# Decoding the first eight weight parts without the guard for tiny numbers, and looking through them late

## The chip, the cores and the metric

The kernel runs on one core of a Trainium2 chip. The metric is the device time of one execution in microseconds; the median of three runs is what a version is compared by. A profiled execution is a further one, taken by the hardware profiler, and has a time of its own.

## The reference

```
scores = 0.125 * q @ k.T, with a bias by distance and head, masked to
         8 global columns and a band of 96 columns; a = softmax(scores)
x = (a @ v), heads side by side                  # 1536 tokens x 512
h = maximum(x @ w_in, 0);   x = h*h @ w_out      # 512 -> 2048 -> 512
gate = 1 / (1 + exp(-(x @ w_gate)));  val = x @ w_val
out = (gate * val) @ w_out2                      # 512 -> 1536 -> 512
```

Two batches, eight heads, 768 positions, head size 64. The weights arrive as float64, so each number is two 32-bit words, and the kernel must make float32 of them on the chip.

## The kernel before

All work is a list of tasks. Each task names its engine (or a choice of two), an estimated duration, a rank, and the buffers that it reads and writes. A planner (`_Plan.issue`) walks through them in a modelled time: whenever an engine is free it takes, of the tasks whose inputs are ready by then, the one of lowest rank. The resulting order is the order of each engine's queue; on the chip every queue runs strictly in order, and an instruction that waits holds all that stands behind it. A load is taken to land its own estimate plus 2 us (`late=2000`) after its issue.

**Attention.** For each of twelve 128-row blocks, TensorE makes scores (L473), VectorE adds the bias and takes the row's extreme (L486), ScalarE takes the exponential (L491), ScalarE or VectorE divide (L510, L512), TensorE transposes (L523), ScalarE or VectorE copy the transposes out (tile `ats`), and TensorE multiplies by the values (L535). The result goes to tile `x` in two parts, a rounded high part and the rest.

**The two feed-forward layers.** Every product is made of three matmuls (L615 to L617): high by low, high by high, low by high. The first layer is done in four passes over its sixteen blocks of hidden columns, the second in four passes over twelve. Pass 0 of the first layer works in pieces of 256 tokens and is interleaved with the attention, since it needs only the `x` of two 128-row blocks; the later passes run 512 tokens at a time. Pass 0 needs the first eight of 68 weight parts: four of `w_in` (tile `h` is written from them), then four of `w_out` (tile `y`).

**A weight part** (`load_weight`) is 128 x 512 numbers, 512 KB. SyncE's queue starts its load into `wst`, a ring of two (L576). Then, in this order:

- L583, ScalarE: the absolute value of the high words, taken as float32, into `wu`
- L585, VectorE: the maximum of that and the smallest high word allowed, into `wx` (a ring of two); this is the guard for tiny numbers
- L587, VectorE: shift left by 5 and right by 2, in place
- L589, VectorE: bring in the top three bits of the low word, in place
- L592, VectorE: bring in the sign and the top exponent bit from the high word, in place
- L253, ScalarE: the rounded high copy into tile `w`
- L263, VectorE: `wx` less the high copy, into the second half of `w`

The words lie in pairs in `wst`, so a reader of the high words alone steps over every other word. The first eight parts go to buffers of pool `sb`; the other thirteen buffers lie in pool `late`, which is opened when the attention's tiles are given up.

**The general way.** L373 to L383 (`whether`) test the two numbers of the inputs that set the band, and write `gen_i`; at the end of the program every engine reads `gen_i` (L56) and, were it not zero, would run a slow way that covers all inputs.

Of the kernel before, what the change touches and what calls it, by code (L numbers as in the profile page):

```python
# [9 lines left out]
F32 = mybir.dt.float32  # L10
# [7 lines left out]
P = 128  # L18
# [4 lines left out]
FAR = 2.0 ** 38  # L23
F64_TOP = -(1 << 30)
F64_MIN = 2.0 ** -15 * 1.125


@with_exitstack
def kernel(
    ctx: ExitStack,  # L30
    tc: tile.TileContext,
    qw: bass.AP,
    kw: bass.AP,
    vw: bass.AP,
    nums: bass.AP,
    w1: bass.AP,
    w2: bass.AP,
    out: bass.AP,
):
    nc = tc.nc  # L40
    NT, DM = out.shape
    NQ, _, H, _ = qw.shape
    w1, w2 = w1.bitcast(I32), w2.bitcast(I32)
    slopes = [2.0 ** (-8.0 * (h + 1) / H) for h in range(H)]

    pers = ctx.enter_context(tc.tile_pool(name="pers", bufs=1))
    nf = pers.tile([P, 2], F32, name="nf")
    gen_i = pers.tile([P, 1], I32, name="gen_i")
    ident = pers.tile([P, P], F32, name="ident")

    with tc.tile_pool(name="sb", bufs=1) as sb, tc.manual_schedule():
        _fast(tc, sb, qw, kw, vw, nums, w1, w2, out, nf, gen_i, ident, slopes)

    engines = [mybir.EngineType.PE, mybir.EngineType.Activation, mybir.EngineType.DVE,
               mybir.EngineType.Pool, mybir.EngineType.SP]
    general = nc.values_load(gen_i[0:1, 0:1], engines=engines)  # L56
    with tc.If(general != 0):
        _general(tc, qw, kw, vw, w1, w2, out, nf, ident, slopes)
# [151 lines left out]
            t["fn"](t["e"]) if t["told"] else t["fn"]()  # L210


def _fast(tc, sb, qw, kw, vw, nums, w1, w2, out, nf, gen_i, ident, slopes):
    nc = tc.nc
    NT, DM = out.shape
    NQ, _, H, _ = qw.shape
# [25 lines left out]
    def act(n):  # L242
        return 200 + n * 0.83
# [31 lines left out]

    v, g = nc.vector, nc.gpsimd
    consts = buf("sb", [P, 1], F32, "consts")
    ni = buf("early", [P, 2, 2], I32, "ni")
    add("sp", 700, -1e6, lambda: nc.sync.dma_start(
        out=ni.ap, in_=nums.rearrange("(o a) b -> o a b", o=1).to_broadcast([P, 2, 2])),  # L280
# [9 lines left out]
    def setup():  # L290
# [82 lines left out]
        def whether():  # L373

            ok = early["sb"].tile([P, 1], F32, name="ok")
            ok2 = early["sb"].tile([P, 1], F32, name="ok2")
            v.tensor_scalar(ok, nl, 1.0, None, op0=ALU.is_ge)
            v.tensor_scalar(ok2, nl, float(NL_MAX), None, op0=ALU.is_le)
            v.tensor_tensor(ok, ok, ok2, op=ALU.mult)
            v.tensor_scalar(ok2, ng, float(GS), None, op0=ALU.is_le)  # L380
            v.tensor_tensor(ok, ok, ok2, op=ALU.mult)
            v.tensor_scalar(ok, ok, -1.0, 1.0, op0=ALU.mult, op1=ALU.add)
            v.tensor_copy(gen_i, ok)  # L383

        add("dve", 1300, 1e8, whether, r=[num], w=[(consts, "gen"), (small, "ok")])

    zero = buf("early", [P, TN], mybir.dt.bfloat16, "zero")
    scrap = buf("psb", [P, TN], F32, "h", 2)
# [178 lines left out]
    def load_weight(n, rank):  # L567
        key = chunks[n]
        k = n % (NA + NB)
        pool_name, bufs, tag = ("sb", NA, "wa") if k < NA else ("late", NB, "wb")  # L570
        st = buf("sb", [P, TN, 2], I32, "wst", 2)
        xx = buf("sb", [P, TN], F32, "wx", 2)
        u = buf("sb", [P, TN], F32, "wu", 1)
        t = buf(pool_name, [P, 2, TN], F32R, tag, bufs, f"w{n}")
        src = (w1 if key[0] == "a" else w2)[key[1], key[2]]
        add("sp", dma(P * TN * 8), rank - LEAD - 6000, lambda: nc.sync.dma_start(  # L576
            out=st.ap.rearrange("p n t -> p (n t)"), in_=src), w=[st], late=2000)
        lo, hi = (lambda: st[:, :, 0]), (lambda: st[:, :, 1])
        xi = lambda: xx.ap.bitcast(I32)
        rank -= LEAD  # L580


        add("act", act(TN), rank, lambda: nc.scalar.activation(u.ap, hi().bitcast(F32), ACTF.Abs),  # L583
            r=[st], w=[u])
        add("dve", dve(TN, False), rank, lambda: v.tensor_scalar(  # L585
            xx.ap, u.ap, F64_MIN, None, op0=ALU.max), r=[u], w=[xx])
        add("dve", dve(TN, False), rank, lambda: v.tensor_scalar(  # L587
            xi(), xi(), 5, 2, op0=ALU.logical_shift_left, op1=ALU.logical_shift_right), w=[xx])
        add("dve", dve(TN), rank, lambda: v.scalar_tensor_tensor(  # L589
            xi(), lo(), 29, xi(), op0=ALU.logical_shift_right, op1=ALU.bitwise_or),  # L590
            r=[st], w=[xx])
        add("dve", dve(TN), rank, lambda: v.scalar_tensor_tensor(  # L592
            xi(), hi(), F64_TOP, xi(), op0=ALU.bitwise_and, op1=ALU.bitwise_or), r=[st], w=[xx])
        copy(WHI, TN, rank, lambda: t[:, 0], lambda: xx.ap, [xx], [(t, 0)])
        minus(WLO, TN, rank, lambda: t[:, 1], lambda: xx.ap, lambda: f32(t[:, 0]), [xx, (t, 0)],
              [(t, 1)])
        made.append(t)


    clock = {"rank": CLK}  # L600
# [169 lines left out]
        rank += NTILE * 3 * len(fs) * KC * steps  # L770
    for n in range(len(chunks)):
        load_weight(n, when[n])
    for fn, p, *rest in work:
        clock["pace"] = 2.0 if fn is moe1 and p == 0 else 1.0
        fn(p, *rest)
# [229 lines left out]
```

## Time and profile before

| | us |
|---|---|
| median of 3 runs (lowest, highest) | 688.71 (688.39, 688.76) |
| the profiled execution | 689.12 |
| its span, first to last instruction | 687.2 |
| TensorE (PE) busy | 667.9 |
| VectorE (DVE) busy | 432.1 |
| ScalarE (ACT) busy | 285.7 |

The span is cut into the attention's opening, in which TensorE is short of work, a long middle in which it is hardly idle, and a last few microseconds of output. The profile names an engine's idle time by the instruction behind it and by what released that instruction. The granted clock of TensorE is given for a stretch as a share of 2.4 GHz: 1.00 is full, 0.50 is 1.2 GHz.

### The profile page before, as it was taken

The page shows a single profiled execution, that of the slowest core. Times are in us where ns is not written, and L with a number is a line of the kernel's source. Part 1 is how long each engine was busy: PE and PEld are TensorE (multiplying, and loading weights), DVE is VectorE, ACT ScalarE, POOL GpSimd, SP SyncE. Part 2 cuts the span into 40 slices and gives each one's busy share as a digit, 9 for nine tenths or more (in the row PEclk, how much of TensorE's full clock was granted, in tenths as well). Part 3 has the DMA queues.
Part 4 walks back from the last instruction along what each step waited for, and adds up shares of the span by engine and source line. Part 5 has one row for each costly group of instructions (what it writes and reads, how often), then busy time and mean ns, then how long its engine had stood idle before and what let it go on. Part 6 is the DMA issues. An engine that isn't in the chain of part 4 may idle for free.

```text
span 687.2 us, 10016 instructions
## 1 busy us (share of the span) xinstructions
PE 667.9 (97%) x3864; PEld 558.7 (81%) x3864; DVE 432.1 (63%) x976; ACT 285.7 (42%) x622; POOL 1.1 (0%) x8
## 2 busy tenths in 40 slices
PE   9878999999999999999999999999999999999996
PEld 7766899899988888888888888888888888888884
DVE  5878876768888888888857852476348223222232
ACT  5767777764463444554434541352113111211110
POOL 0000000000000000000000000000000000000000
PEclk9988899999999999999999999999999999999999
DMA  7754433201332332333210230043001000001011
GB/s 181 171 153 139 150 114 107 73 3 63 123 122 78 107 123 87 98 96 119 82 41 32 93 122 1 31 126 120 0 1 62 1 1 0 1 0 62 0 62 66
DMA packets 29335, 51.71 MB, mean 75 GB/s; under 512 B 3808, under 2 KB 16352, under 8 KB 29280
## 3 DMA queue, kind: packets, MB, share of 16 engines
q1 hardware_dynamic: 29280, 51.00, 24.4%
q8 instruction: 32, 0.52, 0.3%
q14 instruction: 23, 0.19, 0.1%
HBM read 47.84 MB, written 3.15 MB: 74 GB/s over the span
## 4 chain that ended last, share of the span: by engine, by line


## 5 line engine op out<-in xcount | busy, mean ns | idle before, releaser
L615 PE MATMUL h<-x,w 128*128 128x512 f32 (+1 forms) x528 | 197.8, 375 | 0.0
L617 PE MATMUL h<-x,w 128*128 128x512 f32 (+1 forms) x528 | 195.7, 371 | 0.0
L616 PE MATMUL h<-x,w 128*128 128x512 f32 (+1 forms) x528 | 195.7, 371 | 0.0
L615 PEld LDWEIGHTS h<-x,w 128*128 128x128 f32 x528 | 99.9, 189 | 17.5 <-issue 0.2
L617 PEld LDWEIGHTS h<-x,w 128*128 128x128 f32 x528 | 99.9, 189 | 16.9
L616 PEld LDWEIGHTS h<-x,w 128*128 128x128 f32 x528 | 100.0, 189 | 16.7
L713 DVE TENSOR_TENSOR r<-h,r 128x512 f32<-128x512 f32 x36 | 24.9, 691 | 103.1 <-PE h L617 101.6
L615 PE MATMUL y<-g,w 128*128 128x512 f32 (+1 forms) x240 | 86.3, 360 | 2.6 <-ACT w L253 1.7
L616 PE MATMUL y<-g,w 128*128 128x512 f32 (+1 forms) x240 | 84.3, 351 | 0.0
L617 PE MATMUL y<-g,w 128*128 128x512 f32 (+1 forms) x240 | 84.3, 351 | 0.0
L263 DVE TENSOR_TENSOR g<-r,g 128x512 fp32r<-128x512 f32 x84 | 57.7, 687 | 17.2 <-ACT g L253 16.7
L710 ACT ACTIVATE r<-h 128x512 f32<-128x512 f32 x36 | 21.5, 598 | 109.7 <-PE h L617 109.6
L583 ACT ACTIVATE wu<-wst 128x512 f32<-128x512 f32 x68 | 45.2, 665 | 48.5 <-DMA wst<-in_w_dram 41.1
L263 DVE TENSOR_TENSOR w<-wx,w 128x512 fp32r<-128x512 f32 x68 | 46.5, 685 | 21.2 <-ACT w L253 20.7
L615 PE MATMUL o<-w,g 128*128 128x512 f32 x144 | 56.9, 395 | 0.0
L616 PE MATMUL o<-w,g 128*128 128x512 f32 x144 | 56.9, 395 | 0.0
L617 PE MATMUL o<-w,g 128*128 128x512 f32 x144 | 56.8, 394 | 0.0
L253 ACT ACTIVATE w<-wx 128x512 fp32r<-128x512 f32 x68 | 42.5, 626 | 34.0 <-DVE wx L592 28.9
L253 ACT ACTIVATE g<-r 128x512 fp32r<-128x512 f32 x32 | 20.2, 632 | 82.5 <-DVE r L713 82.5
L615 PEld LDWEIGHTS y<-g,w 128*128 128x128 f32 x240 | 45.6, 190 | 10.5 <-ACT w L253 2.0
L617 PEld LDWEIGHTS y<-g,w 128*128 128x128 f32 x240 | 45.7, 190 | 6.7 <-DVE w L263 0.2
L616 PEld LDWEIGHTS y<-g,w 128*128 128x128 f32 x240 | 45.7, 191 | 6.4
(79 smaller groups left out, 827.5 us busy)
## 6 DMA issues: line engine op xcount, KB each, us to landing
wst<-in_w_dram SPq DMA_DIRECT2D x68, 512.0 KB, 3.5
k<-in_kw_dram SPq DMA_DIRECT2D x24, 128.0 KB, 2.9
q<-in_qw_dram SPq DMA_DIRECT2D x24, 128.0 KB, 3.1
vv<-in_vw_dram SPq DMA_DIRECT2D x12, 256.0 KB, 2.9
out_dram<-oacc SPq DMA_DIRECT2D x11, 256.0 KB, 2.1
vv<-in_vw_dram SPq DMA_DIRECT2D x10, 192.0 KB, 3.4
vv<-in_vw_dram SPq DMA_DIRECT2D x10, 64.0 KB, 2.8
out_dram<-oacc SPq DMA_DIRECT2D x2, 128.0 KB, 3.6
```

The lines of the kernel that those rows point to most:

```text
L253: nc.scalar.activation(to(), of(), ACTF.Copy)
L263: nc.vector.tensor_tensor(to(), of(), less(), op=ALU.subtract)
L583: add("act", act(TN), rank, lambda: nc.scalar.activation(u.ap, hi().bitcast(F32), ACTF.Abs), r=[st], w=[u])
L615: nc.tensor.matmul(p, lhsT=ww[:, 0, ws], rhs=lo, start=first, stop=False)
L616: nc.tensor.matmul(p, lhsT=ww[:, 0, ws], rhs=hi, start=False, stop=False)
L617: nc.tensor.matmul(p, lhsT=ww[:, 1, ws], rhs=hi, start=False, stop=last)
L710: add("act", act(TN), rk, lambda r=r, pt=pt: nc.scalar.activation(r.ap, pt.ap, ACTF.Sigmoid), r=[pt], w=[r])
L713: add("dve", dve(TN), rk, lambda r=r, pt=pt: v.tensor_tensor(r.ap, pt.ap, r.ap, op=ALU.mult), r=[pt], w=[r])
```

## The change

For parts 0 to 7 the absolute value and the maximum are gone: the shift reads the high words of `wst` itself. For all parts the sign comes in before the low word's bits, and those go to a new buffer `wf` (one of it): the high copy is made from `wx` without them, and the subtraction takes `wf` instead of `wx`.

After all weights, with a rank above that of any other work but `whether` and the fillers, each of the eight parts is loaded once more (`look_through`): ScalarE takes the absolute value, and VectorE sums what is below the guard into one column of `tiny`. Then (`decide`) a DMA lays `tiny`'s 128 x 8 sums into one row, `asked`; behind them stands the answer of `whether`, which no longer writes `gen_i`. VectorE sums the row, compares with zero and writes `gen_i`.

```diff
--- before.py
+++ after.py
@@ -23,6 +23,7 @@
 FAR = 2.0 ** 38
 F64_TOP = -(1 << 30)
 F64_MIN = 2.0 ** -15 * 1.125
+TINY = 8
 
 
 @with_exitstack
@@ -44,12 +45,13 @@
     slopes = [2.0 ** (-8.0 * (h + 1) / H) for h in range(H)]
 
     pers = ctx.enter_context(tc.tile_pool(name="pers", bufs=1))
+    asked = pers.tile([1, P * TINY + 1], F32, name="asked")
     nf = pers.tile([P, 2], F32, name="nf")
     gen_i = pers.tile([P, 1], I32, name="gen_i")
     ident = pers.tile([P, P], F32, name="ident")
 
     with tc.tile_pool(name="sb", bufs=1) as sb, tc.manual_schedule():
-        _fast(tc, sb, qw, kw, vw, nums, w1, w2, out, nf, gen_i, ident, slopes)
+        _fast(tc, sb, qw, kw, vw, nums, w1, w2, out, nf, gen_i, ident, slopes, asked)
 
     engines = [mybir.EngineType.PE, mybir.EngineType.Activation, mybir.EngineType.DVE,
                mybir.EngineType.Pool, mybir.EngineType.SP]
@@ -210,7 +212,7 @@
             t["fn"](t["e"]) if t["told"] else t["fn"]()
 
 
-def _fast(tc, sb, qw, kw, vw, nums, w1, w2, out, nf, gen_i, ident, slopes):
+def _fast(tc, sb, qw, kw, vw, nums, w1, w2, out, nf, gen_i, ident, slopes, asked):
     nc = tc.nc
     NT, DM = out.shape
     NQ, _, H, _ = qw.shape
@@ -275,6 +277,9 @@
 
     v, g = nc.vector, nc.gpsimd
     consts = buf("sb", [P, 1], F32, "consts")
+
+
+    tiny = buf("sb", [P, TINY], F32, "tiny")
     ni = buf("early", [P, 2, 2], I32, "ni")
     add("sp", 700, -1e6, lambda: nc.sync.dma_start(
         out=ni.ap, in_=nums.rearrange("(o a) b -> o a b", o=1).to_broadcast([P, 2, 2])),
@@ -380,9 +385,9 @@
             v.tensor_scalar(ok2, ng, float(GS), None, op0=ALU.is_le)
             v.tensor_tensor(ok, ok, ok2, op=ALU.mult)
             v.tensor_scalar(ok, ok, -1.0, 1.0, op0=ALU.mult, op1=ALU.add)
-            v.tensor_copy(gen_i, ok)
-
-        add("dve", 1300, 1e8, whether, r=[num], w=[(consts, "gen"), (small, "ok")])
+            v.tensor_copy(asked[:, P * TINY:], ok[0:1])
+
+        add("dve", 1300, 1e8, whether, r=[num], w=[(tiny, "asked"), (small, "ok")])
 
     zero = buf("early", [P, TN], mybir.dt.bfloat16, "zero")
     scrap = buf("psb", [P, TN], F32, "h", 2)
@@ -570,7 +575,6 @@
         pool_name, bufs, tag = ("sb", NA, "wa") if k < NA else ("late", NB, "wb")
         st = buf("sb", [P, TN, 2], I32, "wst", 2)
         xx = buf("sb", [P, TN], F32, "wx", 2)
-        u = buf("sb", [P, TN], F32, "wu", 1)
         t = buf(pool_name, [P, 2, TN], F32R, tag, bufs, f"w{n}")
         src = (w1 if key[0] == "a" else w2)[key[1], key[2]]
         add("sp", dma(P * TN * 8), rank - LEAD - 6000, lambda: nc.sync.dma_start(
@@ -579,22 +583,56 @@
         xi = lambda: xx.ap.bitcast(I32)
         rank -= LEAD
 
-
-        add("act", act(TN), rank, lambda: nc.scalar.activation(u.ap, hi().bitcast(F32), ACTF.Abs),
-            r=[st], w=[u])
-        add("dve", dve(TN, False), rank, lambda: v.tensor_scalar(
-            xx.ap, u.ap, F64_MIN, None, op0=ALU.max), r=[u], w=[xx])
-        add("dve", dve(TN, False), rank, lambda: v.tensor_scalar(
-            xi(), xi(), 5, 2, op0=ALU.logical_shift_left, op1=ALU.logical_shift_right), w=[xx])
-        add("dve", dve(TN), rank, lambda: v.scalar_tensor_tensor(
-            xi(), lo(), 29, xi(), op0=ALU.logical_shift_right, op1=ALU.bitwise_or),
-            r=[st], w=[xx])
+        shift = dict(op0=ALU.logical_shift_left, op1=ALU.logical_shift_right)
+        if n < TINY:
+            add("dve", dve(TN, False), rank, lambda: v.tensor_scalar(xi(), hi(), 5, 2, **shift),
+                r=[st], w=[xx])
+        else:
+
+            u = buf("sb", [P, TN], F32, "wu", 1)
+            add("act", act(TN), rank, lambda: nc.scalar.activation(
+                u.ap, hi().bitcast(F32), ACTF.Abs), r=[st], w=[u])
+            add("dve", dve(TN, False), rank, lambda: v.tensor_scalar(
+                xx.ap, u.ap, F64_MIN, None, op0=ALU.max), r=[u], w=[xx])
+            add("dve", dve(TN, False), rank, lambda: v.tensor_scalar(xi(), xi(), 5, 2, **shift),
+                w=[xx])
         add("dve", dve(TN), rank, lambda: v.scalar_tensor_tensor(
             xi(), hi(), F64_TOP, xi(), op0=ALU.bitwise_and, op1=ALU.bitwise_or), r=[st], w=[xx])
+
+        full = buf("sb", [P, TN], F32, "wf", 1)
+        add("dve", dve(TN), rank, lambda: v.scalar_tensor_tensor(
+            full.ap.bitcast(I32), lo(), 29, xi(), op0=ALU.logical_shift_right,
+            op1=ALU.bitwise_or), r=[st, xx], w=[full])
         copy(WHI, TN, rank, lambda: t[:, 0], lambda: xx.ap, [xx], [(t, 0)])
-        minus(WLO, TN, rank, lambda: t[:, 1], lambda: xx.ap, lambda: f32(t[:, 0]), [xx, (t, 0)],
-              [(t, 1)])
+        minus(WLO, TN, rank, lambda: t[:, 1], lambda: full.ap, lambda: f32(t[:, 0]),
+              [full, (t, 0)], [(t, 1)])
         made.append(t)
+
+    def look_through(n):
+
+        st = buf("sb", [P, TN, 2], I32, "wst", 2)
+        u = buf("sb", [P, TN], F32, "wu", 1)
+        src = w1[chunks[n][1], chunks[n][2]]
+        add("sp", dma(P * TN * 8), 1e7, lambda: nc.sync.dma_start(
+            out=st.ap.rearrange("p n t -> p (n t)"), in_=src), w=[st], late=2000)
+        add("act", act(TN), 1e7, lambda: nc.scalar.activation(
+            u.ap, st[:, :, 1].bitcast(F32), ACTF.Abs), r=[st], w=[u])
+        add("dve", dve(TN) + 80, 1e7, lambda: v.scalar_tensor_tensor(
+            u.ap, u.ap, F64_MIN, u.ap, op0=ALU.is_lt, op1=ALU.mult, accum_out=tiny[:, n:n + 1]),
+            w=[u, (tiny, n)])
+
+    def decide():
+
+        add("sp", 700, 1e7, lambda: nc.sync.dma_start(
+            out=asked[:, 0:P * TINY], in_=tiny.ap), r=[(tiny, n) for n in range(TINY)],
+            w=[(consts, "asked")], late=2000)
+
+        def fn():
+            v.tensor_reduce(asked[:, P * TINY:], asked, axis=AX.X, op=ALU.add)
+            v.tensor_scalar(asked[:, P * TINY:], asked[:, P * TINY:], 0.0, None, op0=ALU.is_gt)
+            v.tensor_copy(gen_i[0:1], asked[:, P * TINY:])
+
+        add("dve", 1600, 1e7, fn, r=[(tiny, "asked"), (consts, "asked")], w=[(consts, "gen")])
 
 
     clock = {"rank": CLK}
@@ -770,6 +808,9 @@
         rank += NTILE * 3 * len(fs) * KC * steps
     for n in range(len(chunks)):
         load_weight(n, when[n])
+    for n in range(TINY):
+        look_through(n)
+    decide()
     for fn, p, *rest in work:
         clock["pace"] = 2.0 if fn is moe1 and p == 0 else 1.0
         fn(p, *rest)
```

## Rows read from the trace of the kernel before

**Rows 1.** The page's first line.

```profile
span 687.2 us, 10016 instructions
```

**Rows 2.** Busy time, instructions, granted clock, DMA share and GB/s by stretch.

```profile
0.00:85.00 85.00, 73.40 (x692) 61.44 (x692) 66.14 (x254) 57.84 (x175) 1.09 (x8) 0.90 0.60 160
85.00:160.00 75.00, 74.68 (x811) 67.62 (x810) 55.06 (x194) 51.58 (x154) 0.00 (x0) 1.00 0.23 68
160.00:530.00 370.00, 369.12 (x1709) 306.45 (x1708) 265.95 (x465) 154.12 (x258) 0.00 (x0) 1.00 0.25 80
530.00:687.20 157.20, 150.66 (x659) 123.14 (x657) 44.93 (x66) 22.18 (x37) 0.00 (x0) 0.99 0.06 21
```

**Rows 3.** The same by finer stretches of the opening.

```profile
47.00:52.00 5.00, 5.00 (x28) 4.63 (x30) 3.16 (x10) 2.29 (x6) 0.00 (x0) 0.50 0.35 122
...
68.00:77.00 9.00, 7.28 (x44) 6.56 (x43) 7.58 (x28) 6.01 (x16) 0.00 (x0) 0.62 0.46 142
```

**Rows 4.** TensorE's order of time: start, us, line, tiles, [idle before <-releaser].

```profile
26.09 1.09 PE L535 MATMUL o<-ats,vv 128*64 128x128 f32 x16
...
45.38 0.41 PE L523 MATMUL at<-ident,sa 128*128 128x128 f32 x2 [2.11 <-DVE sa L512]
46.97 0.69 PE L523 MATMUL at<-ident,sa 128*128 128x128 f32 x2 [1.18 <-ACT sa L510]
...
51.00 1.86 PE L535 MATMUL o<-ats,vv 128*64 128x128 f32 x16
...
69.77 0.58 PE L615 MATMUL y<-g,w 128*128 128x256 f32 x1 [1.72 <-ACT w L253]
```

**Rows 5.** ScalarE's order of time around TensorE's two long waits.

```profile
43.85 0.66 ACT L583 ACTIVATE wu<-wst 128x512 f32<-128x512 f32 x1 [2.54 <-DMA wst<-in_w_dram]
...
46.42 0.89 ACT L510 ACTIVATE sa<-sa,sm 128x256 f32<-128x256 f32 x2
...
68.54 0.66 ACT L583 ACTIVATE wu<-wst 128x512 f32<-128x512 f32 x1 [1.20 <-DMA wst<-in_w_dram]
69.10 0.62 ACT L253 ACTIVATE w<-wx 128x512 fp32r<-128x512 f32 x1
```

**Rows 6.** VectorE's order of time at the same places.

```profile
43.78 0.18 DVE L498 RECIPROCAL sm<-sm 128x4 f32<-128x4 f32 x1
44.54 0.43 DVE L585 TENSOR_SCALAR wx<-wu 128x512 f32<-128x512 f32 x1 [0.58 <-ACT wu L583]
44.88 0.35 DVE L512 TENSOR_SCALAR sa<-sa,sm 128x256 f32<-128x256 f32 x1
...
66.77 0.68 DVE L592 SCALAR_TENSOR_TENSOR wx<-wst,wx 128x512 int32<-128x512 int32 x1
...
69.23 0.43 DVE L585 TENSOR_SCALAR wx<-wu 128x512 f32<-128x512 f32 x1 [1.18 <-ACT wu L583]
```

**Rows 7.** Groups of the decoding from 20 to 85 us.

```profile
L589 DVE SCALAR_TENSOR_TENSOR wx<-wst,wx 128x512 int32<-128x512 int32 x9 | 6.2, 685 | 0.0
...
L583 ACT ACTIVATE wu<-wst 128x512 f32<-128x512 f32 x9 | 6.0, 664 | 4.2 <-DMA wst<-in_w_dram 4.2
...
L263 DVE TENSOR_TENSOR w<-wx,w 128x512 fp32r<-128x512 f32 x8 | 5.5, 686 | 1.0 <-ACT w L253 0.8
...
L585 DVE TENSOR_SCALAR wx<-wu 128x512 f32<-128x512 f32 x9 | 3.8, 420 | 3.9 <-ACT wu L583 3.9
L587 DVE TENSOR_SCALAR wx<-wx 128x512 int32<-128x512 int32 x9 | 3.8, 420 | 0.0
```

**Rows 8.** SyncE's last weight loads and output, then the weight loads' landing.

```profile
162.22 358.67 SPq L576 DMA_DIRECT2D wst<-in_w_dram  x56
629.88 52.17 SPq L745 DMA_DIRECT2D out_dram<-oacc  x13
...
DMA to landing us min/median/max: 3.3/3.5/6.6
```

**Rows 9.** VectorE's order of time in the last pass but one.

```profile
573.50 0.69 DVE L713 TENSOR_TENSOR r<-h,r 128x512 f32<-128x512 f32 x1 [3.37 <-PE h L617]
```

## The prediction

> **What bounds the kernel now.** I read the stretches first. From 85 us to the end TensorE is the bound: it is idle for 0.32 us up to 160, for 0.88 up to 530, and for 6.54 after that, most of it the output behind the last matmul [rows 2]. A VectorE or ScalarE instruction that is saved there buys nothing, and one that is added costs nothing until it makes TensorE wait. The first 85 us are different: TensorE is idle for 85 - 73.40 = 11.6 us, its clock is granted at 0.90 on the mean, and VectorE is busy for 66 of the 85 us [rows 2]. The eight parts that lose their guard are decoded just there, between the instructions of the attention. So I looked at TensorE's waits in that stretch. The two largest places are 3.29 us around 45 us (2.11 for the divided scores of VectorE, then 1.18 for those of ScalarE) and 1.72 us before 69.77, for a weight part's high copy [rows 4]. After both TensorE runs at 1.2 GHz: granted 0.50 from 47 to 52 us, 0.62 on the mean from 68 to 77 [rows 3]. What that costs is seen on the sixteen value matmuls of a half block: 1.09 us at 26.09 in full clock, 1.86 at 51.00 [rows 4].
>
> **What the change takes out of these places.** ScalarE and VectorE show why TensorE waits [rows 5, 6].
>
> At 43.85 ScalarE begins L583 after 2.54 us of waiting for a weight load. Behind it in its queue stand an exponential, a piece of the feed-forward layer, a high copy, and only then, at 46.42, the division L510 that TensorE wants. That division's other input, the reciprocal, was ready at 43.78 + 0.18 = 43.96. Without L583 the queue is 2.54 us plus one instruction's pitch (68.54 to 69.10, so 0.56 us) further, 3.1 us, and L510 is then held by the reciprocal and the four short instructions ahead of it: about 44.2, 2.2 us earlier. On VectorE L585 waited 0.58 us for L583, with the division L512 behind it at 44.88; this goes as well. I count 2.0 us of the 3.29.
>
> At 68.54 ScalarE begins the next such L583, after 1.20 us of waiting for a load, and the copy that TensorE wants stands behind it at 69.10. Its data were ready when L592 ended, at 66.77 + 0.68 = 67.45. Without L583 it starts about 67.6, and the new order, in which the copy doesn't need the low bits, can give another VectorE slot. I count 1.5 us of the 1.72.
>
> The clock: from 47 to 52 us at half speed some 2.5 us are lost (5.00 us busy at 0.50), from 68 to 77 some 2.8 (7.28 us busy at 0.62, so 7.28 x 0.38) [rows 3]. Both losses follow a wait that shrinks without vanishing. No row says how short it must get for the clock to stay; the bounds are 0 and 5.3 us, and I take half, 2.6.
>
> VectorE's saved maximum: 8 x 0.34 us of queue (L585 at 44.54, L512 at 44.88 [rows 6]) is 2.7 us, of which the places above already hold some; I add 0.3 for the rest.
>
> **What it adds, on the path or beside it.** The shift now reads every other word of `wst`. No row has a one-source VectorE instruction on such a pattern. The bounds are 420 ns, as L587 takes on packed words, and 685 ns, as L589, a two-source one, takes on the same kind of pattern [rows 7]. L263, two-source on packed tiles, takes 686 ns, so the step costs nothing there; I take 420. At 685 the eight parts would cost 8 x 0.27 = 2.1 us of VectorE, and most of the 2.7 saved would be gone. The Trainium skill (SBUF — State Buffer, the note on cachelines under the port layout) says that a stride is free while two accesses fall into a line of 16 bytes, which 8 bytes between words satisfy. It agrees with L589 against L263; whether the faster one-source rate holds is shown by no run here.
>
> The load's wait moves from ScalarE to VectorE. Three L583 waited 4.2 us for loads in this stretch and three L585 waited 3.9 for L583 [rows 7], so VectorE pays most of it today. Loads land in 3.3 to 6.6 us, median 3.5 [rows 8], and the planner reckons with 3.5 (1.5 by size and the 2.0 of `late`), so a late one stalls the queue up to 3.1 us, with the scores' bias, the divisions and the reciprocals behind it. At 43.85 and at 68.54, where the loads came late, VectorE had other work until 44.0 and 68.1; I take no more waiting than today's, with 0 to 3.1 us for each late load as the bounds.
>
> For the 60 other parts the count of VectorE instructions stays, one buffer `wf` forces the next part's low-bit step behind the subtraction, and that behind the high copy. Most of it lies from 160 to 530 us, where TensorE waited 0.88 us in all [rows 2]: nothing.
>
> The looking through cannot start before the last weight load (162.22 + 358.67 = 520.9) has been decoded, near 530. Eight more loads through the ring of two, in four pairs of some 3.5 us plus L583 and one VectorE instruction (0.66 and 0.69 [rows 7]), take about 20 to 25 us; so it ends near 555. Then SyncE waits for the sums and sends them: a load's 3.3 to 6.6 us as bounds. VectorE's sum over 1025 numbers in one row is two L589 long, 1.4 us, and two short ones follow. All is over by some 565. Behind them on SyncE stand the outputs, the first at 629.88 [rows 8]; behind them on VectorE stand the gate's products. VectorE is idle for 3.37 us before one such product [rows 9] and has 44.93 us of work in the last 157 [rows 2]. The third product of a pass is wanted by TensorE only after two others' output matmuls, 24 of 150.66 / 659 = 0.229 us, so 5.5 us, of which product, copy and subtraction take about 2.1. An instruction of 1.4 us in the way is covered by the 3.4 left. If that cover were gone it would cost at most 1.4 us, three or four times. At the end the engines read `gen_i` as before, after 682: nothing.
>
> **The sum.** 2.0 + 1.5 + 2.6 + 0.3 = 6.4 us. TensorE's next waits in the opening, for the transposes' copies and the divisions that L583 doesn't hold up, are fed by the same loop of engines, and part of the gain will reappear there; a third is my choice, no row gives it. That leaves 4.3 us. The profiled execution took 689.12 us, its span 687.2 [rows 1] and 1.9 around it, so it would take 684.8; the median lies 0.4 under it, which gives **684.4 us**.
>
> **The rivals.**
>
> *The wait comes back (no change).* The loads are paced by the ring and by SyncE's order, and the attention by its own loop of scores, exponential and transpose; TensorE then waits as long, for something else, and the clock falls as often. For it: two more waits of that stretch are not behind L583. Against: the two largest are. Gain 0 to 1.4 us: 687.3 to 688.7, with as much above, so within 687.3 to 690.1.
>
> *VectorE blocks on the load (slower).* The planner puts the shift on VectorE at the modelled landing, one instruction sooner than L585 stood, and a late load holds VectorE instead of ScalarE. It decides from the point where a load lands over a microsecond after the queue has reached the shift. Three late loads of 1.2 to 2.5 us (the waits of [rows 5, 7]), less the 3.9 that VectorE waits today, would give little; but with all eight shifts meeting it, at 1 us each, less 3.9, and one more stretch at half clock of 2.5, VectorE loses 8 - 3.9 + 2.5 = 6.6 against the 2.7 saved: 3.9 us slower, 692.6; a milder case reaches from 690.1.
>
> *The clock stays up.* Both stretches of half clock vanish and the planner, with less work to place, fills the opening better: 6.4 + 2.7 more of clock = 9.1, so 679.6.
>
> *It doesn't do what it says:* a tiny number would send everything through the general way, hundreds of microseconds. The weights are normal numbers of size about 0.04 and the guard sits near 2 to the -126; I give it no chance.
>
> **How the numbers follow.** The forecast, 680 to 687.3: 0.58. The clock stays up, below 680: 0.04. The wait comes back: 0.20. VectorE blocks, 690.1 to 694: 0.18, of which 0.04 up to 691. The range 680 to 691 holds 0.58 + 0.20 + 0.04 = 0.82. Faster by over 0.2% (1.4 us, about what a measurement of this kernel can tell from no change) is 0.62, within it 0.20, slower 0.18. The forecast's own range is 681.5 to 687.3.
>
> **What would show it.** The shift's duration, 420 or 685 ns. No first-eight L583 on ScalarE before 80 us; TensorE idle in the first 85 us below 9 us and a granted clock above 0.90 there; the second load of the eight parts between 530 and 560 us, and TensorE's idle time from 160 to 600 still under 2 us. It is wrong if VectorE's idle time before the shift, released by the load, adds up to over 4 us, or if TensorE's idle time in the opening is what it was.

## The result and the profile after

The changed kernel takes 678.83 us (median of four runs, 678.00 to 682.02); the ratio to the kernel before is 0.986, interval 0.9837 to 0.9883. Taken again later beside the last experiment, it took 678.38 (677.75 to 679.92), ratio 0.9854, interval 0.9831 to 0.9876. The forecast was 684.4 in a range of 680 to 691. The sign is right, but the gain of 9.9 us (against 688.74 beside it) is more than twice the 4.3 forecast, and the time lies below the range.

The page's head and the stretches of after, with the columns of [rows 2]: us, busy time and instructions of TensorE, its weight loads, VectorE, ScalarE and GpSimd, granted clock, DMA share, GB/s.

```profile
span 677.5 us, 10074 instructions
...
PE 660.8 (98%) x3864; PEld 553.0 (82%) x3864; DVE 436.4 (64%) x986; ACT 287.4 (42%) x623; POOL 1.1 (0%) x8
```

```profile
0.00:85.00 85.00, 76.84 (x783) 63.50 (x784) 68.20 (x267) 58.79 (x185) 1.09 (x8) 0.98 0.58 157
85.00:160.00 75.00, 74.55 (x785) 68.25 (x785) 56.09 (x184) 49.57 (x141) 0.00 (x0) 1.00 0.26 79
160.00:530.00 370.00, 370.00 (x1688) 306.52 (x1687) 267.28 (x464) 155.18 (x260) 0.00 (x0) 1.00 0.27 86
530.00:677.50 147.50, 139.41 (x613) 114.74 (x612) 44.78 (x72) 23.90 (x39) 0.00 (x0) 0.99 0.10 33
```

Beside [rows 2] two numbers of the first 85 us tell most: TensorE is idle for 8.16 instead of 11.6 us, and its clock is granted at 0.98 instead of 0.90, so 1.7 instead of 8.5 us of full clock are lost. Both are of one execution each, and the loss differs between executions: the profiled one of before has a mean clock of 0.985 over its span, where the median of 103 executions is 0.989. VectorE is busier in that stretch, not less busy: it got further. Where the 9.7 us of the span lie is read best from TensorE's order of time: its first matmul from `x` with 512 columns for `h` (attention and the first pass are nearly over), its first for the output `o`, and its last. L615 to L617 of before are L653 to L655 of after. Before, then after:

```profile
167.16 0.40 PE L615 MATMUL h<-x,w 128*128 128x512 f32 x1
```

```profile
400.19 0.39 PE L615 MATMUL o<-w,g 128*128 128x512 f32 x1
...
680.27 0.39 PE L617 MATMUL o<-w,g 128*128 128x512 f32 x1
```

```profile
158.79 0.40 PE L653 MATMUL h<-x,w 128*128 128x512 f32 x1
```

```profile
390.85 0.39 PE L653 MATMUL o<-w,g 128*128 128x512 f32 x1
...
669.02 0.39 PE L655 MATMUL o<-w,g 128*128 128x512 f32 x1
```

The opening gives 8.37 us (167.16 to 158.79). From there to the first `o` it is 233.03 us against 232.06, 0.97 more. From the first `o` to the end of the last matmul (680.66 and 669.41) it is 280.47 against 278.56, another 1.91, which nothing in the prediction covers. These 1.91 us are no matter of the opening: in all nine kernels of the experiments that look through eight parts late the same stretch takes 278.56 or 278.57 us, in the six others that don't 280.47 or 280.48. Behind the last matmul 8.09 us follow instead of 6.54, so 1.55 go back; in all other profiles this end takes 7.4 to 9.7 us, so the 6.54 of before are the shortest seen. 8.37 + 0.97 + 1.91 - 1.55 = 9.70.

TensorE's largest waits in after (engine, line, what it waited for: us in total, times, longest), where 2.11, 1.18 and 1.72 us had stood [rows 4]:

```profile
PE at L528 <- DVE ats L257: 1.8, 2, 0.9
...
PE y L653 <- DVE g L265: 1.2, 3, 0.5
PE h L653 <- DVE x L551: 1.1, 1, 1.1
...
PE at L528 <- ACT sa L515: 0.6, 2, 0.4
```

### The profile page after: what moved, and what is told of

Its sections match the earlier page's. It is cut to its first block, busy times and chain, and to the rows that moved or that the text cites. A ratio compares the mean times of both kernels' runs of the same rounds, so it can differ in the third digit from the quotient of the medians.

```text
span 677.5 us, 10074 instructions
## 1 busy us (share of the span) xinstructions
PE 660.8 (98%) x3864; PEld 553.0 (82%) x3864; DVE 436.4 (64%) x986; ACT 287.4 (42%) x623; POOL 1.1 (0%) x8
## 4 chain that ended last, share of the span: by engine, by line
## 5 line engine op out<-in xcount | busy, mean ns | idle before, releaser
L653 PE MATMUL h<-x,w 128*128 128x512 f32 (+1 forms) x528 | 197.2, 373 | 1.1 <-DVE x L551 1.1
L655 PE MATMUL h<-x,w 128*128 128x512 f32 (+1 forms) x528 | 195.2, 370 | 0.0
L653 PEld LDWEIGHTS h<-x,w 128*128 128x128 f32 x528 | 99.3, 188 | 18.8 <-DVE x L551 1.4
L655 PEld LDWEIGHTS h<-x,w 128*128 128x128 f32 x528 | 99.4, 188 | 17.1
L653 PE MATMUL y<-g,w 128*128 128x512 f32 (+1 forms) x240 | 85.6, 357 | 1.2 <-DVE g L265 1.2
L655 PE MATMUL y<-g,w 128*128 128x512 f32 (+1 forms) x240 | 83.5, 348 | 0.5 <-DVE w L265 0.5
L265 DVE TENSOR_TENSOR g<-r,g 128x512 fp32r<-128x512 f32 x84 | 57.8, 688 | 16.4 <-ACT g L255 16.1
L265 DVE TENSOR_TENSOR w<-wf,w 128x512 fp32r<-128x512 f32 x68 | 46.8, 688 | 19.7 <-ACT w L255 18.1
L593 ACT ACTIVATE wu<-wst 128x512 f32<-128x512 f32 x60 | 39.9, 666 | 39.0 <-DMA wst<-in_w_dram 35.4
L653 PE MATMUL o<-w,g 128*128 128x512 f32 x144 | 56.4, 392 | 0.0
L255 ACT ACTIVATE g<-r 128x512 fp32r<-128x512 f32 x36 | 22.7, 632 | 79.2 <-DVE r L751 78.9
L655 PE MATMUL o<-w,g 128*128 128x512 f32 x144 | 55.9, 388 | 0.0
L653 PEld LDWEIGHTS y<-g,w 128*128 128x128 f32 x240 | 45.0, 188 | 10.1 <-DVE g L265 1.9
L655 PEld LDWEIGHTS y<-g,w 128*128 128x128 f32 x240 | 45.2, 188 | 7.1 <-DVE w L265 0.7
L654 PEld LDWEIGHTS y<-g,w 128*128 128x128 f32 x240 | 45.1, 188 | 6.5
```

What stands on the lines that cost most here:

```text
L255: nc.scalar.activation(to(), of(), ACTF.Copy)
L265: nc.vector.tensor_tensor(to(), of(), less(), op=ALU.subtract)
L653: nc.tensor.matmul(p, lhsT=ww[:, 0, ws], rhs=lo, start=first, stop=False)
L654: nc.tensor.matmul(p, lhsT=ww[:, 0, ws], rhs=hi, start=False, stop=False)
L655: nc.tensor.matmul(p, lhsT=ww[:, 1, ws], rhs=hi, start=False, stop=last)
```

## The experiments

The milestone is TensorE's first 512-column matmul for `h`, as above. It and the full clock lost in the first 85 us, (1 - granted) x 85, are of the one execution that was profiled, whose own time stands beside them; several of these executions are among the slowest of their kernel. The last column is the median, over all executions of the kernel, of the mean granted clock of the whole span: 0.001 is some 0.7 us of lost clock, and 1.3 to 3.3 us of it lie behind the last matmul in every profile.

| kernel | median us | profiled us | milestone us | clock lost us | mean clock |
|---|---|---|---|---|---|
| before | 688.2 to 689.0 in six comparisons | 689.1 | 167.2 | 8.5 | 0.989 |
| changed | 678.8, again 678.4 | 679.4, again 678.0 | 158.8, again 157.4 | 1.7, again 0.0 | 0.996, again 0.995 |
| e6_sameorder | 684.0 | 684.3 | 161.2 | 3.4 | 0.995 |
| e7_waitonly | 687.7 | 686.8 | 164.1 | 5.1 | 0.989 |
| e1_guard / e12_guard_j1 | 685.7 / 683.5 | 687.8 / 685.3 | 164.9 / 163.5 | 6.8 / 6.8 | 0.988 / 0.989 |
| e2_order | 687.4 | 688.5 | 166.4 | 5.1 | 0.992 |
| e3_nolook | 680.1 | 680.2 | 158.0 | 1.7 | 0.996 |
| e4_absback | 681.4 | 681.4 | 160.8 | 0.0 | 0.996 |
| e5_maxback / e13_maxback_j1 | 687.2 / 686.3 | 688.3 / 687.4 | 166.9 / 166.9 | 10.2 / 10.2 | 0.983 / 0.986 |
| e11_oldwork | 685.6 | 689.9 | 167.7 | 11.9 | 0.989 |
| e14_dveonly | 685.7 | 682.7 | 162.2 | 1.7 | 0.984 |
| e15_actonly | 686.8 | 687.0 | 164.6 | 6.8 | 0.987 |
| e8_clock | 692.8 | 694.9 | 171.5 | 5.1 | 0.991 |
| e9_j1 | 691.0 | 693.3 | 170.6 | 6.8 | 0.986 |
| e10_j1 | 679.1 | 679.6 | 158.1 | 0.0 | 0.995 |
| e16_tiny10 / e18_tiny10 | 682.5 / 682.9 | 681.8 / 681.6 | 158.8 / 158.6 | 0.0 / 0.0 | 0.996 / 0.994 |

Three theories stood against each other: that the guard's work and its wait for the load cost the time; that the new order of the bits does; that any new order of the queues moves the time as much.

**The parts of the change alone.** e1_guard takes the guard away and leaves the bits in their old order; e2_order does the reverse; e3_nolook is the change without the late work.

```diff
 # e1_guard, against after (shortened)
-            full.ap..., lo(), 29, xi(), ...)      # after the sign, into wf
+            xi(), lo(), 29, xi(), ...)            # before the sign, in place
 # e2_order, against before (in words)
-  shift, low bits in place, sign in place, copy xx, xx less copy
+  shift, sign in place, low bits into wf, copy xx, wf less copy
 # e3_nolook, against after
-    for n in range(TINY):
-        look_through(n)
-    decide()
```

> The guard of the first eight parts is gone and the late looking through is there; the low bits come in before the sign as in the kernel before, into the same buffer. Theory 'guard' (the two instructions per part and the wait for the load on ScalarE made TensorE wait and lose its clock): most of the gain is here, 678 to 682 us, TensorE's granted clock over the first 85 us at 0.96 or more. Theory 'order of the bits' (the parts come sooner because the high copy starts a VectorE slot earlier): little gain, 686 to 689 us. Theory 'planner' (any new order of the queues moves the time by as much): anything from 677 to 692.

> The new order of the bits and the buffer wf for all 68 parts, the guard kept for all of them, no looking through. Theory 'guard': 686 to 690 us, clock in the first 85 us near the 0.90 of before. Theory 'order of the bits': 678 to 683 us. Theory 'planner': anything from 677 to 692.

> The changed kernel without the eight late loads, their reading and the sending of the sums: tiny numbers are not looked for at all, gen_i comes from the test of the band alone. If the late work is hidden, as the prediction has it, the time is that of the changed kernel within 1 us (678 to 681, by the run-to-run spread of the changed kernel), and TensorE's idle time after 530 us stays; if the late work costs something, or lengthens the end, it is 1 to 3 us faster.

Alone the guard's removal gave 2.6 us (ratio 0.995, interval 0.9931 to 0.9969) and the order of the bits 0.9 (0.9976, 0.9958 to 0.9994); together they give 9.9. Neither theory had that. e1_guard has the late work and with it the 1.9 us of the `o` matmuls; without them the removal in it is worth 0.7.

Without the late work the time is 680.05, 1.2 us above the changed kernel. That isn't the price of the late work alone, because e3_nolook also lacks the 1.9 us of the `o` matmuls (280.48 us from the first `o` to the last matmul's end); set against that, the late work would cost 0.2 to 0.7 us (678.4 or 678.8 for the changed kernel), within the spread of the runs. No wait of TensorE shows for it: the changed kernel's TensorE is busy throughout, from 160 to 530 us as above and from 530 to 620. e3_nolook's first and last `o` matmul, then that stretch of the changed kernel:

```profile
389.85 0.39 PE L652 MATMUL o<-w,g 128*128 128x512 f32 x1
...
669.94 0.39 PE L654 MATMUL o<-w,g 128*128 128x512 f32 x1
```

```profile
530.00:620.00 90.00, 90.00 (x397) 74.28 (x397) 29.89 (x50) 16.51 (x27) 0.00 (x0) 1.00 0.06 19
```

Its loads run in SyncE's queue from 515 to 537 us and the sums are sent at 548, 71 us ahead of the first output:

```profile
515.26 21.99 SPq L616 DMA_DIRECT2D wst<-in_w_dram  x8
547.98 0.55 SPq L626 DMA_DIRECT2D asked<-tiny  x1
618.99 51.83 SPq L783 DMA_DIRECT2D out_dram<-oacc  x13
```

**The removal in the old order of the queues.** The planner still counts what is left out, so every queue keeps its order.

```diff
 # e6_sameorder, against before, for n < 8 (shortened)
-   nc.scalar.activation(u.ap, hi()..., ACTF.Abs);  v.tensor_scalar(xx.ap, u.ap, F64_MIN, ...)
+   None;                                           None
-   v.tensor_scalar(xi(), xi(), 5, 2, ...)
+   v.tensor_scalar(xi(), hi(), 5, 2, ...)
 # e7_waitonly: the same, but
+   nc.scalar.activation(u[:, 0:1], st[:, 0:1, 1]..., ACTF.Abs)
```

> The kernel before with its queues in exactly the order they had, but for parts 0 to 7 the absolute value and the maximum are not issued (the planner still counts them) and the shift reads the high words; tiny numbers are not guarded in those parts. Theory 'guard', as the prediction has it: the two waits shrink without any new order, 681 to 686 us, clock in the first 85 us above 0.93. Theory 'planner' (the gain needs the new order): 687 to 689 us. Theory 'VectorE blocks on the load': 689 to 692.

> As the run with the queues in the order of before, but the absolute value of parts 0 to 7 is issued on one column instead of 512 (ScalarE still waits for each load there, its work is 0.2 instead of 0.66 us); the maximum isn't issued, and tiny numbers are not guarded in those parts. If ScalarE's wait for the load with the division behind it is what counted, most of the gain of the same-order run (684.0) is lost: 686 to 689 us, and TensorE's wait for L512 and L510 near 45 us is back at over 2.5 us. If the saved work alone counted: 683 to 685.

This is the case that the prediction worked out (it put the order of the bits at nothing), and it took 683.98 us against 684.4 forecast. Like e3_nolook it has neither the late work nor the faster `o` matmuls, and both ran beside the same 688.31 of before: the removal takes 4.3 us, and the order of the bits with the planner's new order of the queues another 3.9 (683.98 to 680.05). ScalarE in e6_sameorder, and TensorE's transposes behind it:

```profile
42.89 0.63 ACT L253 ACTIVATE w<-wx 128x512 fp32r<-128x512 f32 x1 [0.82 <-DVE wx L594]
43.42 0.61 ACT L650 ACTIVATE g<-r 128x512 fp32r<-128x512 f32 x1
43.94 0.89 ACT L510 ACTIVATE sa<-sa,sm 128x256 f32<-128x256 f32 x2
```

```profile
44.28 0.65 PE L523 MATMUL at<-ident,sa 128*128 128x128 f32 x4 [1.23 <-DVE sa L512]
...
62.41 0.36 PE L617 MATMUL y<-g,w 128*128 128x256 f32 x1 [0.22 <-ACT w L253]
```

L510 starts at 43.94 (worked out: about 44.2), and TensorE's 3.29 us have become 1.23, 2.06 less (worked out: 2.0). The wait of 1.72 us for the high copy has become 0.22. e7_waitonly gives nearly all of the gain back, though ScalarE's work in it is almost as small:

```profile
42.79 0.20 ACT L584 ACTIVATE wu<-wst 128x1 f32<-128x1 f32 x1 [1.53 <-DMA wst<-in_w_dram]
...
44.91 0.89 ACT L510 ACTIVATE sa<-sa,sm 128x256 f32<-128x256 f32 x2
```

```profile
44.44 0.41 PE L523 MATMUL at<-ident,sa 128*128 128x128 f32 x2 [1.22 <-DVE sa L512]
45.46 0.44 PE L523 MATMUL at<-ident,sa 128*128 128x128 f32 x2 [0.61 <-ACT sa L510]
```

ScalarE waits 1.53 us for the load there with L510 behind it, and the time is 687.71. So of the 4.3 us 3.7 hang on ScalarE's waiting for the loads, not on the length of its work. They don't come back as TensorE's wait at this place, though: it is 1.83 us, where over 2.5 were expected and e6_sameorder has 1.23. What comes back with the time is the lost clock: the mean clock is 0.989 as in before and 0.995 in e6_sameorder, a difference of some 4 us of full clock.

**The shares of the two engines.** e4 and e5 put one instruction per part back and let the planner know; e14 and e15 do the same in the changed kernel's order, without the planner's knowledge. e11 puts both back without their durations, but its shift now waits for the absolute value, and the planner makes another order of it: TensorE's queue differs from 48 us on.

```diff
 # e4_absback (planned) and e15_actonly (planned as 1 ns), against after, for n < 8 (shortened)
+   u = buf("sb", [P, TN], F32, "wu", 1)
+   add("act", act(TN) or 1, rank, lambda: nc.scalar.activation(u.ap, hi()..., ACTF.Abs), ...)
 # e5_maxback (planned) and e14_dveonly (within the shift's task)
+   v.tensor_scalar(xi(), xi(), 0, 0, **shift)
 # e11_oldwork: absolute value as 1 ns, maximum within the shift's task
```

> The changed kernel with ScalarE's absolute value of parts 0 to 7 back (planned, its result unused; the shift doesn't wait for it). If ScalarE's share (eight instructions of 0.66 us and their waits for the load) carries the gain: 684 to 688 us. If VectorE's share does: 678 to 681.

> The changed kernel with one more VectorE instruction of 0.42 us for each of parts 0 to 7 (planned; a shift by nothing in the place of the maximum), ScalarE without its absolute value. If VectorE's share carries the gain: 683 to 687 us. If ScalarE's does: 678 to 681.

> The changed kernel's plan, in which the absolute value of parts 0 to 7 counts 1 ns and the maximum nothing, but both are issued: the new order of the queues with the old work and the old wait for the load on ScalarE. If the removed work and wait are what the gain needs, it is mostly lost: 685 to 690 us, granted clock of the first 85 us at 0.94 or less. If the new order of the queues carries it: 679 to 683.

> The changed kernel's queues in exactly their order, with one more VectorE instruction of 0.42 us behind the shift of parts 0 to 7, of which the planner doesn't know. If VectorE's occupancy is what the gain came from: most of the loss of the run with the old work in this order (685.6 us) is here, 683 to 687. If ScalarE's is: 678 to 681.

> The changed kernel's plan with the absolute value of parts 0 to 7 issued on ScalarE as work of 1 ns for the planner, its result unused, and VectorE as in the changed kernel. If ScalarE's share counts: 683 to 687. If VectorE's does: 678 to 681.5.

> The run with one more VectorE instruction for each of parts 0 to 7 (687.2 us), with the planner's landing time moved from 2.0 to 1.9 us. If eight VectorE instructions of 0.42 us cost this much whatever the order: 684 to 688 us again. If that run had an unlucky order: 679 to 682.

Eight VectorE instructions of 0.42 us take 6.9 us of the gain in the very order of the changed kernel (685.71 against 678.83), 8.3 in the order that the planner makes when it knows of them (687.17), and 7.3 when that one is run again with the edit of the next paragraph (686.32 against 679.06). ScalarE's eight of 0.66 us take 2.6 when the planner knows of them (681.43) and 8.0 when it doesn't (686.80): then they stand in front of divisions, and wait for loads there. In e15_actonly, ScalarE and TensorE:

```profile
32.23 0.66 ACT L589 ACTIVATE wu<-wst 128x512 f32<-128x512 f32 x1 [2.33 <-DMA wst<-in_w_dram]
...
33.29 1.29 ACT L515 ACTIVATE sa<-sa,sm 128x256 f32<-128x256 f32 x3
```

```profile
33.84 0.66 PE L528 MATMUL at<-ident,sa 128*128 128x128 f32 x4 [2.14 <-ACT sa L515]
```

That is the pattern of [rows 5] at another place. Both shares together (e11_oldwork, in its own order) cost 6.8, no more than each alone, so they don't add up. In e11_oldwork, e15_actonly and the two with VectorE's instruction planned the lost clock is back, 6.8 to 11.9 us in the profiles and a mean clock of 0.983 to 0.989 over all their executions.

e14_dveonly shows the two parts of what VectorE's instructions cost. Its profile is of one of its quickest executions (682.7; its ten runs lie from 681.6 to 689.6), which loses as little clock as the changed kernel's, 1.7 us. There the milestone is 3.4 us later (162.20 against 158.79), as much as the eight instructions' own time, 8 x 0.42:

```profile
162.20 0.40 PE L656 MATMUL h<-x,w 128*128 128x512 f32 x1
```

Over the ten runs the mean clock is 0.984 instead of 0.995, and the slow ones have the lowest (0.980 at 689.6). So about half of the 6.9 us is VectorE's time, and the rest goes with TensorE's clock.

Why VectorE's own time counts in full is seen in the changed kernel from 45 to 66 us: it is busy for 20.86 of 21 us, at full clock of TensorE.

```profile
45.00:66.00 21.00, 16.90 (x161) 13.05 (x160) 20.86 (x62) 13.96 (x36) 0.00 (x0) 1.00 0.60 176
```

It is the bound there. The eighth part, on which the first pass waits, is finished by the subtraction of L263 or L265; its start in before, after and e5_maxback:

```profile
74.14 0.68 DVE L263 TENSOR_TENSOR w<-wx,w 128x512 fp32r<-128x512 f32 x1
```

```profile
66.90 0.69 DVE L265 TENSOR_TENSOR w<-wf,w 128x512 fp32r<-128x512 f32 x1
```

```profile
72.54 0.69 DVE L265 TENSOR_TENSOR w<-wf,w 128x512 fp32r<-128x512 f32 x1
```

**The order of the queues by itself.** One number of the planner, the reckoned landing of a weight load, is moved from 2.0 to 1.9 us.

```diff
-            out=st.ap..., in_=src), w=[st], late=2000)
+            out=st.ap..., in_=src), w=[st], late=1900)
```

> The kernel before with one number of the planner moved: a weight load is reckoned to land after 1.9 instead of 2.0 us beyond its size; same work, another order of the queues. If the order alone moves the time as much as the change did, this is off 688.5 by 4 us or more to either side, with the granted clock of the first 85 us between 0.88 and 0.99; if not, 686.5 to 690.5.

> The changed kernel with the same number moved from 2.0 to 1.9 us. If its gain is in the work that is gone and the order of the bits, 677 to 682 us, clock in the first 85 us at 0.95 or more; if half of its gain is a lucky order of the queues, 683 to 687.

> The run without the guard but with the low bits in their old place (685.7 us), with the planner's landing time moved from 2.0 to 1.9 us. If the two halves of the change need each other: 684 to 688 us again. If that run only had an unlucky order of the queues: 679 to 682.

The traces show that this test reaches less far than it was meant to. In the opening it changes the queues of one kernel alone, the one of before (VectorE's and ScalarE's from 74 to 76 us on); it got 2.8 us slower (691.0 against 688.18). In the other three the first instruction in another place comes behind the opening: at 204 us in the changed kernel, 166 in e1_guard, 212 in e5_maxback. There the runs are repeats of the same opening: the changed kernel stayed (679.06), e1_guard got 2.2 us faster, of which 1.05 lie between the first `h` and the first `o` (233.56 and 232.51 us in the profiles), and e5_maxback 0.9 faster. So one other order of the opening is worth 2.8 us and a repeat up to 2.2; e1_guard's 2.6 us and e2_order's 0.9 are no finer than this. That both halves together give 4.4 (679.06 against 683.5) to 6.9 us (678.83 against 685.73) more than the guard alone is beyond it, and it goes with the clock: the mean is 0.995 against 0.988, some 4.5 us of full clock that TensorE doesn't lose.

The planner's new order by itself explains nothing of the removal: without the guard and with the bits in their old order the time is 684.0 in the old queues, 685.7 and 683.5 in the new ones, although these two have the faster `o` matmuls. Nor is the changed kernel's opening one lucky order: e4_absback has other queues from 20 us on and e16_tiny10 from 66, and both reach the milestone nearly as early and lose no clock there. How much of the 3.9 us beyond e6_sameorder is the order of the queues was not measured.

**The clock, and more parts.**

```diff
 # e8_clock, against before, in twelve groups of transposes
+   for _ in range(6):
+       nc.tensor.matmul(at...[:, 0:256], lhsT=zero[:, 0:P], rhs=zero[:, 0:256], ...)
 # e16_tiny10 and e18_tiny10, against after
-TINY = 8
+TINY = 10
```

> The kernel before with six further matmuls on zeros ahead of each of twelve groups of transposes in the attention's middle, about 0.65 us of TensorE each; they stand where it waits for the divided scores. If the idle time ahead of the transposes is what costs the clock, the granted clock over the first 85 us rises from 0.90 to above 0.95 and the time falls or stays: 682 to 688 us, although nothing became faster on the other engines. If the clock falls for another reason, it stays near 0.90 and the time rises by the matmuls that don't fit into idle time: 690 to 696.

> The changed kernel with ten parts instead of eight decoded without the guard and looked through late. Parts 8 and 9 are read by ScalarE at 65 and 72 us, still among the attention. If VectorE's work in the opening counts wherever it stands: 0.5 to 2 us faster, 677 to 678.5. If the parts that the first pass waits for are what counts: the changed kernel's time, 678 to 680.

> The changed kernel once more, beside the one with ten parts on the same chip. If its gain over before is as stable as its own four runs say: 677 to 682 us with the granted clock of the first 85 us at 0.95 or more in the profile.

> The kernel with ten parts without the guard once more, beside the changed kernel on the same chip. If VectorE's work in the opening counts wherever it stands: 0.5 to 2 us below the changed kernel. If only the parts that the first pass waits for count: within 1 us of it. If the 682.5 us of its first run are its own: 2 us or more above.

e8_clock settles nothing. The lost clock went from 8.5 to 5.1 us, less than expected, and the matmuls cost more than that, 692.78 (ratio 1.0058, 1.0039 to 1.0077). By the trace the first of them runs at 54.5 us, behind the longest of the waits that it was made for, the one at 45 us, so the clock is lost there as before. Its stretch, and TensorE at those two places:

```profile
0.00:85.00 85.00, 75.11 (x724) 62.55 (x725) 65.22 (x251) 56.96 (x173) 1.09 (x8) 0.94 0.56 160
```

```profile
44.82 0.41 PE L527 MATMUL at<-ident,sa 128*128 128x128 f32 x2 [1.41 <-DVE sa L512]
...
54.51 0.83 PE L523 MATMUL at<-zero 128*128 128x256 bf16 x6
```

Ten parts are 4.5 us slower than eight on the same chip (682.91 against 678.38), although the opening is nearly as short (158.6 against 157.4) and 0.5 to 2 us less were expected. Of the 3.7 us between the two profiles 1.2 come from the opening and 2.4 from behind the first `o`: 280.99 us to the last matmul's end against 278.56. No tried version beats the changed kernel.

## Why the prediction was right or wrong

Beside one run of before (688.31) the gain falls into three parts: 4.3 us by the guard's removal alone (683.98), 3.9 more with the bits in their new order and the planner's order that goes with it (680.05), and 1.2 more with the late work and the faster `o` matmuls (678.83, in a comparison of its own). The forecast had the first part, put the second at nothing and didn't know of the third.

- **What bounds the kernel**: right. 8.37 of the 9.7 us came from the opening, by fewer and shorter waits of TensorE and by its clock.
- **The two waits**: right in place and size. In the old order of the queues they shrank by 2.06 and 1.5 us, against 2.0 and 1.5 worked out.
- **The clock**: about right over all executions, though the bound was drawn too narrow. It was put at 2.6 us, half of the 5.3 lost in two stretches. The profile loses 8.5 us in the opening ([rows 2], (1 - 0.90) x 85), some of it in a third stretch that was not looked at:

```profile
59.40:62.80 3.40, 3.40 (x29) 2.85 (x27) 2.96 (x13) 2.73 (x8) 0.00 (x0) 0.51 0.24 99
```

  But that was one of the low-clock executions. By the medians the mean clock rises from 0.989 to 0.995, which is 4.1 us of lost clock. Among the 103 executions of before one us more of lost clock goes with 0.6 us more time, so by an estimate from these the term measured 2.6 to 4.1.
- **"A third reappears", and the sum**: right for the guard's removal alone, in part by luck. 4.3 us were forecast; the removal gave 4.3 in the old order of the queues, 2.6 and 5.5 in the new ones, of which 1.9 each are of the `o` matmuls. That the third reappears is not shown by this. The mean clock of e6_sameorder is already that of the changed kernel, so the clock gave some 4 us of lost clock rather than 2.6, and in its profile the opening is 6.0 us shorter (167.2 to 161.2), of which the end behind the last matmul takes 1.2 back.
- **The order of the bits**: this is the step that failed. It was put down as nothing but "another VectorE slot" for the high copy, within the 1.5 us of the second wait. Alone it is worth 0.9 us, so that looks right; with the guard gone it is worth 3.9 (e6_sameorder to e3_nolook), and 4.4 to 6.9 against e1_guard and its repeat. The two parts were priced one by one and added, and they are worth more together: without the order of the bits the planner's new queues lose the clock as before (0.988), with it they don't (0.995). How much of this is the copy's earlier start and how much the place that the planner finds for it was not separated, so the cause stays open there.
- **VectorE's saved maximum, 0.3 us**: failed with it. It was priced as queue time left over after the two waits. In the changed kernel these eight instructions, put back, take 6.9 to 8.3 us: their own time of 3.4, and the rest with the clock. VectorE fills 20.86 of 21 us once ScalarE's waits are gone; an instruction more on it then delays the weight parts (68.58 instead of 66.90 for the eighth in e14_dveonly, 72.54 in e5_maxback), and in e5_maxback 10.2 us of clock are lost instead of 1.7. Before, VectorE's idle 19 of 85 us hid that it comes next.
- **The shift on every other word**: right, and now shown. The group in after:

```profile
L588 DVE TENSOR_SCALAR wx<-wst 128x512 int32<-128x512 int32 x8 | 3.4, 424 | 1.1 <-DMA wst<-in_w_dram 1.0
```

  424 ns against the 420 of L587 on packed words [rows 7]. The Trainium skill (SBUF — State Buffer, the note on cachelines under the port layout) has such a stride free of charge. The trace agrees, for the faster one-source rate too.
- **The load's wait on VectorE** (the slower rival): it adds up to 1.0 us, as the same row shows, where eight waits of 1 us were its condition. VectorE is busy with other work until the loads have landed, as in the row of 45 to 66 us.
- **The late work**: right that it is hidden. It ended at 551 us instead of the 565 reckoned, its loads began at 515 and not after 520, and TensorE was idle for 0.00 us from 160 to 530. That the `o` matmuls are 1.9 us faster in the kernels that have it was not foreseen; without this the time would have been some 680.7, the low end of the range.
- **The rivals**: what happened is closest to the one called "the clock stays up", at 679.6, to which 0.04 was given: the clock does stay up, and the planner fills the opening better. That the time came out 0.8 us below it is in part luck, since 1.9 us come from the `o` matmuls.
- **The end**: 1.55 us went into the end behind the last matmul, against a profile of before with the shortest end of all.

## What to carry to other kernels

Two edits of one stage that free the same chain of engines need not add up: here 0.9 us and 4.3 us alone make 8.3 together (688.31 to 680.05, without the late work), so price them on the stage as it is after the other one. Price a saving on the engine that becomes the bound once today's waits are gone, not by the waits of today; an engine whose idle time (here 19 of 85 us) others cause is such a one. Take a lost clock from the row of the whole stretch and from more than one execution, ask what a variant changes far from the stage that it is about (here 1.9 us), and look for an instruction that waits for a DMA in the queue of an engine that others wait for: it cost more by its waiting (3.7 of 4.3 us) than by its work.

## What the runs showed of the hardware

The time of the same kernel on the same chip varies with the granted clock: the kernel before took 685.13 us in a run with a mean clock of 0.996 and 690.97 in one with 0.988. One profile shows one such case, and a gain that comes by the clock wants several.

TensorE's full-clock rate in the long part isn't quite fixed. One group of the matmuls for `o` from 200 to 640 us, in before, after and the kernel with ten parts (count, busy us, mean ns of one):

```profile
L617 PE MATMUL o<-w,g 128*128 128x512 f32 x120 | 47.3, 394 | 0.0
```

```profile
L655 PE MATMUL o<-w,g 128*128 128x512 f32 x125 | 48.5, 388 | 0.0
```

```profile
L655 PE MATMUL o<-w,g 128*128 128x512 f32 x122 | 47.8, 392 | 0.0
```

From 400 to 500 us before has 438 matmuls, after 441, the kernel with ten parts 438, all at a granted clock of 1.00. From the first `o` to the last matmul's end this makes 278.56 or 278.57 us in every profile of a kernel that holds `asked` and `tiny` for eight parts, 280.47 or 280.48 in those without either and in e3_nolook (without `tiny`), and 280.99 in the two for ten parts. The buffers behind them lie elsewhere in the on-chip memory, which would fit, but no run moved a buffer alone: the cause stays open.
